# The first search's thresholds, the late parts of w2 and the fourth token plane of an attention and mixture-of-experts kernel

## The chip, the core and the metric

The kernel runs on one core of a Trainium2 chip. The core has five engines that work in parallel, each through its own list of instructions in order: TensorE (PE; its weight loads are PEld), VectorE (DVE), ScalarE (ACT), GpSimd (POOL) and SyncE (SP), which here only issues DMAs. The metric is the device time of one execution in microseconds (us), as the median of several.

## The reference

Attention over 8 batches, 12 heads, 448 tokens and 64 columns a head, then a mixture of 8 experts in which each (token, expert) pair is taken greedily by its logit until an expert has 448 tokens.

```python
scores = cap * np.tanh(scale * np.matmul(q, k.transpose(0, 1, 3, 2)) / cap)
attn = softmax(scores); x = matmul(attn, v)            # 3584 tokens, 768 columns
logits = x @ w_gate                                     # 8 experts
for idx in np.argsort(-logits.flatten()):               # greedy, best first
    tok, e = idx // E, idx % E
    if assigned[tok] >= 0 or counts[e] >= N // E: continue
    assigned[tok] = e; counts[e] += 1
for e in range(E):
    h = np.maximum(x[assigned == e] @ w1[e], 0.0)       # 768 -> 1024
    out[assigned == e] = h @ w2[e]                      # 1024 -> 768
```

## The kernel before, in words

**Two stages.** The first 338 us are attention, with the logits of each batch behind it. Then the experts are found one after another, each by a *search*, and each found expert gets a *pass* p of two matrix products. The first search (`s.cur==0`) runs before any pass; the later ones run beside the passes. The same expert order as in the reference comes out.

**A search** finds three thresholds, one after another: A, B and C, with 5, 6 and 5 steps in the first search. A step (`select`, L498 to L517) has three thresholds and counts how many of the 3584 x 8 candidates (128 x 224) lie below each: ACT takes one threshold (`cmpA`, L501, a Sign with a sum), DVE two (`cmpD`, L504, a compare with a sum). PE sums the counts over the partitions (L509), DVE adds up the terms of the row whose counts are within the limit (`fl`, L513), which gives the new base `th`, and then writes the next row of thresholds as base plus constants (`r_HA` from `r_CA`, L517). During the first search, ACT also evacuates the transposed rows of the last attention batches (`raw`, L50), POOL scales them (`xn`, L53) and SP stores them to `xs` in DRAM. The end of a search is a chain on DVE: `wt`, `wB`, `sx` (L573 to L578), then the expert's number `ei` (L612), and, at its end, `zz` (L658) behind which POOL gathers the expert's 448 rows (L789, four gathers of 128 rows, the last of 64). PE keeps itself busy meanwhile with small matmuls into a spare PSUM tile `psX` (`warm`, L714, columns 0 to 127).

**Proposals** (L449 to L468, DVE) make from the logits the next candidates `r_VA`, `r_VB`, `r_VC` and `r_K` for the search that follows; PE turns them (L478) and DVE moves the turned ones to SBUF (L483).

**A pass** is 320 ticks, one for each matmul: 144 for `ffn1` (8 blocks of 18, line L869), then 176 for `ffn2` (u=0 to 7: 24, 24, 24 and 16 matmuls, twice, line L900). Float32 values are cut into a high part (`w1h`, `w2h`, `xgh`: ACT, L760 or L821) and a low part (`w1l`, `w2l`: POOL, L764; `xgl`: POOL L828 or DVE L823); PE multiplies high by high, high by low and low by high. `cut` issues both parts. A pass needs eight parts of w2, n=0 to 7; the early ones are cut during `ffn1`, the rest (n=5, 6, 7, or only 7 for p=2) during `ffn2`, at the tick given by the table that the diff shows last. A `gap` memset (L762) stands between two splits of POOL.

**Tokens of the next expert** (for passes from FT=2 on) come in by planes: four ACT copies `pl` (L811) split the gathered rows in 16-bit planes, each is stored to DRAM `xz` (L812, on ACT's DMA queue), and two DMA transposes issued by SP (L815) bring the columns back: the first reads `xz0` (planes 1 and 2), the second `xz1` (planes 3 and 4). Then `cutt` makes `xgh` and `xgl` in four steps.

**The order** of each engine's instructions is the order in which the code is written, with the helpers `tick`, `xq` (a list of things to issue at a due tick) and `bg` (cuts that may be issued in idle time between two bounds) deciding where a piece stands. Nothing reorders it afterwards. A search's steps are issued between the matmuls of a pass by their own rule of ticks.

Of the kernel before, what the change touches and what calls it, by code (L numbers as in the profile page):

```python
# [7 lines left out]
AF=mybir.ActivationFunctionType; ALU=mybir.AluOpType; AX=mybir.AxisListType  # L8
# [324 lines left out]
class Routing:  # L333
# [155 lines left out]
    def select(s,wp,Vt,ab,mid=None,post=None):  # L489
        nc=s.nc; v=nc.vector  # L490
        NV=s.NV; wide=s.cur>1
        R=s.R8[ab] if wide else (4,)*s.steps[ab]
        T0,H,C=(s.T8,s.H8,s.C8) if wide else (s.T0,s.H,s.C)
        T0=T0[ab]; H=H[ab]; C=C[ab]; steps=len(R)
        th=[T0[:,k:k+1] for k in range(R[0]-1)]
        for i in range(steps):
            m=R[i]-1; alone=s.cur>FT and ab=="A" and i<3; na=m if alone else 5 if m==7 else s.na
            cd=(s.cd8 if m==7 else s.cds)[s.nd%3]; s.nd+=1  # L498
            o=wp.tile([128,s.NX],BF16,name="cmpA",bufs=1)
            with nc.allow_low_precision(reason="integers up to 256 are exact in bfloat16"):  # L500
                for k in range(na,m): nc.scalar.activation(o,Vt,AF.Sign,bias=th[k],scale=-1.0,accum_out=cd[:,k:k+1])  # L501
                for k in range(na):
                    o=wp.tile([128,NV],BF16,name="cmpD",bufs=2)
                    with s.tc.issue_after(s.hold) if s.hold else nullcontext(): v.tensor_scalar(o,Vt[:,:NV],th[k],None,op0=ALU.is_lt,op1=ALU.add,accum_out=cd[:,k:k+1])  # L504
            if mid and i<len(mid): mid[i]()
            s.bg()
            s.pos='A'; yield max(6,12-s.since()) if s.cur==1 and s.since()<20 else 16 if m==7 and s.place()>304 else max(13,18-s.since()) if m==7 and s.since()<20 else s.hA+1*(s.cur==1)+(3 if m==7 else 0)+(3 if alone and i else 0); s.pos=''
            ps=s.psum()
            nc.tensor.matmul(ps[:,:m+1],s.bo,cd,start=True,stop=True)  # L509
# [3 lines left out]
            v.scalar_tensor_tensor(fl[:,:m+1],ps[:,:m+1],s.lim,H[:,i,0:m+1],op0=ALU.is_le,op1=ALU.mult,accum_out=t0)  # L513
            if i+1<steps:
                nt=wp.tile([128,1],F32,name="nt",bufs=2)
                m=R[i+1]-1
                v.tensor_scalar(H[:,i+1,m:2*m],C[:,i+1,0:m],t0,None,op0=ALU.add,op1=ALU.add,accum_out=nt)  # L517
                th=[t0]+[H[:,i+1,m+k:m+k+1] for k in range(1,m)]
            if i==steps-1:
                s.tA=t0  # L520
                if ab=="C": s.row(s.tA)
            s.pos='B'; yield s.hB; s.pos=''
    def search(s,wp,turned=()):
        nc=s.nc; v=nc.vector
        post=None
        if turned:
            for h in range(s.NC//16):
                if ("VA",h) not in turned: s.turn("VA",h)
            late=[lambda: s.propose_b(s.NC-4,s.NC,PB(nc)),lambda: None,lambda: s.key(s.NC-4,s.NC)]
            post=lambda: s.flips(s.pm.tile([128,512],F32,name="psM"))  # L530
        else: late,post=s.turns()
# [25 lines left out]
        k2=s.vps[:112,448:448+s.NC]  # L557
# [7 lines left out]
        if s.cur>=EW:  # L565
            yield 4
            s.pw=s.psum()
            nc.tensor.matmul(s.pw[:112,0:16],s.onesf,R,start=True,stop=True)
            s.best(wp,0,s.pw[:112,0:8],k2); s.pw=s.pw[:112,8:16]
        else:  # L570
            s.pw=part[0]; s.warm(4)
        tt=wp.tile([112,8],F32,name="wt")
        v.tensor_tensor(tt,s.pw,s.wm,op=ALU.mult)  # L573
        s.wB=wp.tile([112,1],F32,name="wB")
        v.tensor_reduce(s.wB,tt,axis=AX.X,op=ALU.max)
# [111 lines left out]
def ffn_all(nc, tc, ctx, rt, xs, xz, w1, w2, out, ident, E, wp, deferred, xctx, gen):  # L687
# [20 lines left out]
    m=0  # L708
    wu=[None]; end=[-99]
    def warm(n,t=None):  # L710
# [4 lines left out]
    rt.warm=warm; rt.since=lambda: now[0]-end[0]; rt.place=lambda: now[0]%320  # L715
    warm(9)
    step()
    units(2)
# [31 lines left out]
    def load2(p,n,gate=None):  # L750
# [6 lines left out]
    def cut(key,r,shape,name,bufs,eng=None,view=lambda t:t,use=lambda t:t):  # L757
        h=ws.tile(shape,F32R,name=name+"h",bufs=bufs)
        l=ws.tile(shape,F32R,name=name+"l",bufs=bufs)
        nc.scalar.activation(view(h),r,AF.Copy)  # L760
        if not eng:
            if tt[0]: nc.gpsimd.memset(gap,0.0)  # L762
            lp[0]=False; tt[0]=True
        (eng or nc.gpsimd).tensor_tensor(view(l),r,view(h).bitcast(F32),op=ALU.subtract)  # L764
        spl[key]=(use(h),use(l))
    def split1(p,f,eng=None):
        if p>=E: return
        cut((p,1,f),raw[p,1,f],[128,DC,128],"w1",3,eng)
    def split2(p,n):
        hf,i=order(p)[n]  # L770
        view=use=lambda t:t.rearrange("p (o d) -> p o d",o=2)
        cut((p,2,hf,i),raw[p,2,hf,i],[128,2*HD],"w2",8,None,view,use)
# [35 lines left out]
    def planes(j):  # L808
        o,n=TS[j]; k,r=divmod(j,2)
        pl=fp.tile([128,2,DM],I16,name="pl",bufs=4)  # L810
        nc.scalar.activation(pl[:n],row(j,n).bitcast(I16).rearrange("p (d h) -> p h d",h=2),AF.Copy)  # L811
        nc.scalar.dma_start(xz[k][r*256:r*256+2*n].rearrange("(p h) d -> p h d",h=2),pl[:n])  # L812
        if r:
            n=o+n-2*128*k
            nc.sync.dma_start_transpose(xgp[k][:,:DC*n].bitcast(I16).rearrange("p (c t) -> p c t",c=DC),xz[k])  # L815
    def cutt(p,k,c0,c1):
        newx(p)
        o,n=((0,256),(256,192))[k]
# [20 lines left out]
    def tick(n=1):  # L839
        cnt[0]+=n; bc[0]+=n; now[0]+=n  # L840
        if bc[0]>=BG:
            if pend: bc[0]=0; scatter(*pend.pop(0))
        if len(res)>cur[0]+1 and cur[0]+1 not in xgs:
            bc[0]=0; n=cur[0]+1; gather(n)
            if n>=FT:
                xq.extend((now[0]+TD+TJ*j,lambda j=j: planes(j)) for j in range(4))
                xq.extend(((n-1)*320+248+8*f,lambda f=f: split1(n,f)) for f in range(2))
                o=(n-1)*320; g=now[0]-o; a=max(262,g+92); b=max(284,g+120)
                bg.extend((o+x,o+min(y,316),z) for x,y,z in ((a,a+18,lambda: cutt(n,0,0,3)),(a,a+34,lambda: cutt(n,0,3,6)),(b,b+(4 if n==FT else 26),lambda: cutt(n,1,0,3)),(b,b+22,lambda: cutt(n,1,3,6))))
        while xq and xq[0][0]<=now[0]: xq.pop(0)[1]()  # L850
# [78 lines left out]
    for p in range(E):  # L929
# [22 lines left out]
        for u in range(8):  # L952
# [72 lines left out]
```

## Time and profile before

| what | value |
|---|---|
| median of 3 runs | 896.42 us (895.92 to 897.0) |
| the profiled execution, time and span | 895.64 us, 893.8 us |
| TensorE, mean granted clock | 1.000 |
| PE, share of the span | 96% |
| first search, first to last `fl` | 339.9 to 362.7 us |
| gather of the first expert | 370.3 us |
| `w2l` on POOL | 64 x 1.85 us = 118.0 us |

A row of the profile's views gives start and duration in us, engine, line, operation, the tile written <- the tiles read, shape, and in brackets how long the engine was idle before it and what it waited for. The rows are quoted where the prediction uses them.

### The profile page before, as it was taken

The page shows a single profiled execution, that of the slowest core. Times are in us where ns is not written, and L with a number is a line of the kernel's source. Part 1 is how long each engine was busy: PE and PEld are TensorE (multiplying, and loading weights), DVE is VectorE, ACT ScalarE, POOL GpSimd, SP SyncE. Part 2 cuts the span into 40 slices and gives each one's busy share as a digit, 9 for nine tenths or more (in the row PEclk, how much of TensorE's full clock was granted, in tenths as well). Part 3 has the DMA queues.
Part 4 walks back from the last instruction along what each step waited for, and adds up shares of the span by engine and source line. Part 5 has one row for each costly group of instructions (what it writes and reads, how often), then busy time and mean ns, then how long its engine had stood idle before and what let it go on. Part 6 is the DMA issues. An engine that isn't in the chain of part 4 may idle for free.

```text
span 893.8 us, 17555 instructions
## 1 busy us (share of the span) xinstructions
PE 861.8 (96%) x6198; PEld 629.2 (70%) x6198; DVE 595.9 (67%) x2020; ACT 583.9 (65%) x822; POOL 371.8 (42%) x528
## 2 busy tenths in 40 slices
PE   7899999999999997899999999999999999999997
PEld 4334444444333335788989989989889989999997
DVE  3788988989887888767777677777767772130210
ACT  6988898889899957274383683664645735425521
POOL 8100000000000007574585593683864855856941
PEclk9999999999999999999999999999999999999999
DMA  8799999997995007770931874846926927828601
GB/s 121 114 131 144 129 170 171 142 166 105 213 179 85 1 4 250 237 227 1 314 94 51 247 234 128 253 150 195 285 86 186 283 63 211 284 75 250 205 10 54
DMA packets 336121, 139.61 MB, mean 156 GB/s; under 512 B 258304, under 2 KB 325632, under 8 KB 335520
## 3 DMA queue, kind: packets, MB, share of 16 engines
q1 hardware_dynamic: 326448, 107.96, 55.5%
q0 software_dynamic: 4656, 22.02, 7.2%
q10 hardware_dynamic: 4928, 8.49, 2.6%
q8 instruction: 49, 0.80, 0.4%
q14 instruction: 40, 0.33, 0.1%
HBM read 97.15 MB, written 33.03 MB: 146 GB/s over the span
## 4 chain that ended last, share of the span: by engine, by line
PE 70%; issue 12%; DVE 6%; POOL 4%; DMA 3%; SPq 2%; ACT 2%; POOLq 0%; DVEq 0%; ACTq 0%
PE psH L869 23%; PE psH L900 14%; PE psA L189 12%; PE psS L148 10%; PE psM L206 4%; POOL xg L789 2%; PE psS L153 2%; SPq L92 2%; PE psM L37 1%; DVE es L165 1%; POOL w2l L764 1%; POOL out_dram L882 1%; DVE cmpD L504 1%; DMA xg<-xz 1%; DMA k<-in_k_dram 1%
## 5 line engine op out<-in xcount | busy, mean ns | idle before, releaser
L900 PE MATMUL psH<-w2h,hh 128*128 128x384 f32 x896 | 235.2, 340 | 0.0
L900 PE MATMUL psH<-w2l,hh 128*128 128x384 f32 x512 | 167.5, 341 | 3.6 <-POOL gap L762 3.6
L154 ACT ACTIVATE e<-psS 128x896 f32<-128x896 f32 x168 | 147.5, 909 | 30.8 <-PE psS L148 18.0
L900 PEld LDWEIGHTS psH<-w2h,hh 128*128 128x128 f32 x896 | 161.8, 188 | 0.3
L159 ACT ACTIVATE e<-e,bias 128x1792 f32<-128x1792 f32 (+2 forms) x74 | 147.3, 1991 | 2.0
L869 PE MATMUL psH<-xgh,w1h 128*128 128x448 f32 x384 | 143.2, 373 | 1.0 <-ACT xgh L821 0.7
L869 PE MATMUL psH<-xgh,w1l 128*128 128x448 f32 x384 | 141.4, 368 | 0.0
L148 PE MATMUL psS<-tq,tk 64*64 64x448 f32 x1152 | 129.9, 544 | 7.4 <-ACT e L154 4.8
L869 PE MATMUL psH<-xgl,w1h 128*128 128x448 f32 x384 | 136.7, 369 | 0.0
L764 POOL TENSOR_TENSOR w2l<-w2r,w2h 128x768 fp32r<-128x768 f32 x64 | 118.0, 1846 | 42.7 <-ACT w2h L760 42.7
L460 POOL TENSOR_SCALAR r_Bt<-r_b 112x4 f16<-112x4 int32 x1 | 0.2, 201 | 304.1 <-DVE rin L243 304.1
L764 POOL TENSOR_TENSOR w1l<-w1r,w1h 128x768 fp32r<-128x768 f32 x62 | 114.3, 1845 | 19.0 <-ACT w1h L760 14.3
L189 PE MATMUL psA<-e,nv 64*64 64x448 f32 x1104 | 120.5, 540 | 1.2 <-DVE xT L199 1.2
L165 DVE TENSOR_TENSOR es<-es,e 64x896 f32<-64x896 f32 (+2 forms) x74 | 100.3, 1356 | 2.6 <-ACT e L159 1.3
L900 PEld LDWEIGHTS psH<-w2l,hh 128*128 128x128 f32 x512 | 95.5, 188 | 5.7 <-POOL gap L762 5.6
L148 PEld LDWEIGHTS psS<-tq,tk 64*64 64x64 f32 x1152 | 43.7, 132 | 73.2 <-issue 37.9
L875 ACT ACTIVATE hh<-psH 128x448 fp32r<-128x448 f32 x64 | 34.8, 543 | 86.0 <-PE psH L869 79.7
L877 DVE SCALAR_TENSOR_TENSOR hh<-psH,hh 128x64 fp32r<-128x64 f32 (+1 forms) x128 | 43.9, 385 | 67.0 <-ACT hh L875 66.0
L189 PEld LDWEIGHTS psA<-e,nv 64*64 64x64 f32 x1104 | 46.4, 133 | 59.1 <-issue 49.6
L906 ACT ACTIVATE on<-psH 128x384 f32<-128x384 f32 x48 | 23.4, 487 | 90.2 <-PE psH L900 85.9
L869 PEld LDWEIGHTS psH<-xgh,w1h 128*128 128x128 f32 x384 | 72.5, 189 | 6.6 <-ACT xgh L821 1.0
L869 PEld LDWEIGHTS psH<-xgh,w1l 128*128 128x128 f32 x384 | 72.3, 188 | 5.2
(340 smaller groups left out, 1321.5 us busy)
## 6 DMA issues: line engine op xcount, KB each, us to landing
w1r<-in_moe_w_dram SPq DMA_DIRECT2D x64, 384.0 KB, 4.7
w2r<-in_moe_w_dram SPq DMA_DIRECT2D x64, 384.0 KB, 6.8
k<-in_k_dram SPq DMA_DIRECT2D x92, 112.0 KB, 3.4
q<-in_q_dram SPq DMA_DIRECT2D x92, 112.0 KB, 3.9
nv<-in_v_dram SPq DMA_DIRECT2D x72, 128.0 KB, 3.9
xz<-pl ACTq DMA_DIRECT2D x18, 384.0 KB, 3.0
xs<-xn SPq DMA_DIRECT2D x4, 1344.0 KB, 7.0
xs<-xn SPq DMA_DIRECT2D x4, 896.0 KB, 5.2
```

The lines of the kernel that those rows point to most:

```text
L148: for c in range(2): nc.tensor.matmul(ps[c*64:c*64+64,h,:S],tks[g,0][hp,o,u*128+c*64:u*128+c*64+64],tks[g,1][hp,o,:],start=True,stop=True)
L154: nc.scalar.activation(ev(g,r),ps[:,:,:S],AF.Tanh,scale=sr[0])
L159: act=lambda: nc.scalar.activation(e,e,AF.Exp,scale=sr[1],bias=bias)
L165: t=es_t[g]; add=lambda o,a,b: nc.vector.tensor_tensor(o,a,b,op=ALU.add)
L189: nc.tensor.matmul(avp[g,o][h*64:h*64+64,:S],lhs,rhs[hp,h,:],start=(j==0 and x==0),stop=j==3)
L206: nc.tensor.matmul(ps[g*32:g*32+32,:S],lhs,rhs,start=first,stop=last)
L764: (eng or nc.gpsimd).tensor_tensor(view(l),r,view(h).bitcast(F32),op=ALU.subtract)
L869: nc.tensor.matmul(ps[:,:C],a[:,c,:],b[:,c,:],start=(m==0),stop=(m==DC*3-1)); m+=1
L875: nc.scalar.activation(h[:,:C],ps[:,:C],AF.Relu)
L877: nc.vector.scalar_tensor_tensor(h[:,d:d+b-a],ps[:,a:b],0.0,h[:,a:b].bitcast(F32),op0=ALU.max,op1=ALU.subtract)
L900: nc.tensor.matmul(ps[:,:HD],h[:,f,a:a+128],spl[p,2,hf,f//2][w][:,f%2,:],start=(m==0),stop=(m==nm-1))
L906: if t<3: nc.scalar.activation(ons[p][0][:,t*DM+hf*HD:t*DM+hf*HD+HD],ps[:,:HD],AF.Copy)
```

## The change

It has four parts. (1) The late w2 parts of a pass p>1 are issued earlier: their high parts at ticks 6, 12 and 18 of the first `ffn2` unit (for p=2 the one late part at tick 2 of the second), and their low parts through `xq`, at ticks 188, 198 and 208 of the pass. (2) In the first search, all steps but the first of each pass have DVE subtract the base from the proposals and compare with constants, which ACT copied to columns 128 on of `psX` before the search; the row of thresholds is written behind the compares, and ACT's threshold is now the base itself. (3) The fourth plane's store is issued by SP, and both transposes behind it; the due times of the cuts move by a few ticks. (4) In the later searches `wt` is written to eight spare columns of the PSUM tile that already holds `psR`.

```diff
@@ Routing.select: one pass of a threshold search
+                quick=s.cur==0 and i>0
-                for k in range(na,m): nc.scalar.activation(o,Vt,AF.Sign,bias=th[k],scale=-1.0,accum_out=cd[:,k:k+1])
-                for k in range(na):
+                for k in [0] if quick else range(na,m): nc.scalar.activation(o,Vt,AF.Sign,bias=th[k],scale=-1.0,accum_out=cd[:,k:k+1])
+                for k in range(1,m) if quick else range(na):
                     o=wp.tile([128,NV],BF16,name="cmpD",bufs=2)
+                    if quick:
+                        v.scalar_tensor_tensor(o,Vt[:,:NV],t0,s.cps[ab][:,i,k:k+1].broadcast_to([128,NV]),op0=ALU.subtract,op1=ALU.is_lt,accum_out=cd[:,k:k+1])
+                        continue
...
+            if quick: v.tensor_scalar(H[:,i,m:2*m],C[:,i,0:m],t0,None,op0=ALU.add,op1=ALU.add,accum_out=wp.tile([128,1],F32,name="nt",bufs=2))
...
-                nt=wp.tile([128,1],F32,name="nt",bufs=2)
+                if s.cur: nt=wp.tile([128,1],F32,name="nt",bufs=2)
                 m=R[i+1]-1
-                v.tensor_scalar(H[:,i+1,m:2*m],C[:,i+1,0:m],t0,None,op0=ALU.add,op1=ALU.add,accum_out=nt)
+                if s.cur: v.tensor_scalar(H[:,i+1,m:2*m],C[:,i+1,0:m],t0,None,op0=ALU.add,op1=ALU.add,accum_out=nt)
@@ Routing.search
+        if s.cur==0:
+            ps=s.spare(); s.cps={}; o=128
+            for n in "ABC":
+                S=s.steps[n]; s.cps[n]=ps[:,o:o+3*S].rearrange("p (s k) -> p s k",k=3); o+=3*S
+                nc.scalar.activation(s.cps[n][:,1:],s.C[n][:,1:],AF.Copy)
...
-            s.best(wp,0,s.pw[:112,0:8],k2); s.pw=s.pw[:112,8:16]
+            s.best(wp,0,s.pw[:112,0:8],k2); tt=s.pw[:112,16:24]; s.pw=s.pw[:112,8:16]
         else:
-            s.pw=part[0]; s.warm(4)
-        tt=wp.tile([112,8],F32,name="wt")
+            s.pw=part[0]; s.warm(4); tt=wp.tile([112,8],F32,name="wt")
@@ ffn_all, cut and split2
-        if not eng:
-            if tt[0]: nc.gpsimd.memset(gap,0.0)
-            lp[0]=False; tt[0]=True
-        (eng or nc.gpsimd).tensor_tensor(view(l),r,view(h).bitcast(F32),op=ALU.subtract)
+        def low():
+            if not eng:
+                if tt[0]: nc.gpsimd.memset(gap,0.0)
+                lp[0]=False; tt[0]=True
+            (eng or nc.gpsimd).tensor_tensor(view(l),r,view(h).bitcast(F32),op=ALU.subtract)
+        if at is None: low()
+        else: xq.append((at,low)); xq.sort(key=lambda x: x[0])
@@ ffn_all, planes
-        nc.scalar.dma_start(xz[k][r*256:r*256+2*n].rearrange("(p h) d -> p h d",h=2),pl[:n])
-        if r:
-            n=o+n-2*128*k
-            nc.sync.dma_start_transpose(xgp[k][:,:DC*n].bitcast(I16).rearrange("p (c t) -> p c t",c=DC),xz[k])
+        (nc.sync if j==3 else nc.scalar).dma_start(xz[k][r*256:r*256+2*n].rearrange("(p h) d -> p h d",h=2),pl[:n])
+        if j==3:
+            for k,n in ((0,256),(1,192)): nc.sync.dma_start_transpose(xgp[k][:,:DC*n].bitcast(I16).rearrange("p (c t) -> p c t",c=DC),xz[k])
@@ ffn_all, tick: due times of the cuts of the token columns
-                o=(n-1)*320; g=now[0]-o; a=max(262,g+92); b=max(284,g+120)
-                bg.extend((o+x,o+min(y,316),z) for x,y,z in ((a,a+18,lambda: cutt(n,0,0,3)),(a,a+34,lambda: cutt(n,0,3,6)),(b,b+(4 if n==FT else 26),lambda: cutt(n,1,0,3)),(b,b+22,lambda: cutt(n,1,3,6))))
+                o=(n-1)*320; g=now[0]-o; a=max(262,g+92); b=max(284,g+118)
+                bg.extend((o+x,o+min(y,316),z) for x,y,z in ((a,a+18,lambda: cutt(n,0,0,3)),(a,a+34,lambda: cutt(n,0,3,6)),(b,b+(0 if n==FT else 26),lambda: cutt(n,1,0,3)),(b,b+(7 if n==FT else 22),lambda: cutt(n,1,3,6))))
@@ ffn_all: the late w2 parts of a pass p>1
-                for m,n in ({3:[(2,7)]} if p==2 else {2:[(14,5),(20,6)],3:[(2,7)]}).get(u,()): wk[m]=wk.get(m,[])+[lambda n=n: split2(p,n)]
+                for m,n in ({1:[(2,7)]} if p==2 else {0:[(6,5),(12,6),(18,7)]}).get(u,()): wk[m]=wk.get(m,[])+[lambda n=n: split2(p,n,320*p+138+10*n)]
```

On VectorE, the list around the fourth and fifth step of pass C of the first search: before, and of the change (`psR` is the count from PE, `th` the base, `r_CC` the constants in SBUF, `r_HC` the row, `psX` the PSUM tile).

```order
L513 SCALAR_TENSOR_TENSOR fl,th<-psR,r_HC 128x4
L517 TENSOR_SCALAR r_HC,nt<-r_CC,th 128x3
L504 TENSOR_SCALAR cmpD,r_cd_316<-r_qt,th 128x224
L504 TENSOR_SCALAR cmpD,r_cd_316<-r_qt,r_HC 128x224
L513 SCALAR_TENSOR_TENSOR fl,th<-psR,r_HC 128x4
```

```order
L518 SCALAR_TENSOR_TENSOR fl,th<-psR,r_HC 128x4
L506 SCALAR_TENSOR_TENSOR cmpD,r_cd_316<-r_qt,th,psX 128x224 x2
L509 TENSOR_SCALAR r_HC,nt<-r_CC,th 128x3
L518 SCALAR_TENSOR_TENSOR fl,th<-psR,r_HC 128x4
L506 SCALAR_TENSOR_TENSOR cmpD,r_cd_317<-r_qt,th,psX 128x224 x2
L509 TENSOR_SCALAR r_HC,nt<-r_CC,th 128x3
L518 SCALAR_TENSOR_TENSOR fl,th<-psR,r_HC 128x4
```

The row of thresholds, which stood between `fl` and the compares, stands behind both compares, which no longer read it.

On ScalarE, pass p=3 from the last `hh` of `ffn1` to the first results of the second half: before, and of the change. `pl` are the plane copies, `xz` the planes in DRAM, `on` a result.

```order
L875 ACTIVATE hh<-psH 128x448 x3
L906 ACTIVATE on<-psH 128x384
L811 ACTIVATE pl<-xg_4110 128x1536
L812 DMA xz_62<-pl 128x1536
...
L906 ACTIVATE on<-psH 128x384
L811 ACTIVATE pl<-xg_4111 64x1536
L812 DMA xz_63<-pl 64x1536
L760 ACTIVATE w2h<-w2r 128x768 x2
L906 ACTIVATE on<-psH 128x384
L760 ACTIVATE w2h<-w2r 128x768
```

```order
L886 ACTIVATE hh<-psH 128x448 x3
L769 ACTIVATE w2h<-w2r 128x768 x3
L917 ACTIVATE on<-psH 128x384
L823 ACTIVATE pl<-xg_4113 128x1536
L824 DMA xz_62<-pl 128x1536
...
L824 DMA xz_63<-pl 128x1536
L917 ACTIVATE on<-psH 128x384
L823 ACTIVATE pl<-xg_4114 64x1536
```

Three high parts `w2h` (n=5, 6, 7), which stood behind the fourth copy and its store, stand ahead of the first `on`. POOL's list doesn't change in order: gathers, then the low parts.

On SyncE, the third pass around the transposes: before, and of the change.

```order
L747 DMA w1r<-in_moe_w_dram 128x6x128
L747 ISA
L747 DMA w1r<-in_moe_w_dram 128x6x128
L815 DMA_TRANSPOSE xg_4110<-xz_62 128x6x512
L815 DMA_TRANSPOSE xg_4111<-xz_63 128x6x384
L747 ISA
L747 DMA w1r<-in_moe_w_dram 128x6x128
L755 ISA
```

```order
L756 DMA w1r<-in_moe_w_dram 128x6x128
L756 ISA
L756 DMA w1r<-in_moe_w_dram 128x6x128
L824 DMA xz_63<-pl 64x1536
L826 DMA_TRANSPOSE xg_4113<-xz_62 128x6x512
L826 DMA_TRANSPOSE xg_4114<-xz_63 128x6x384
L756 ISA
```

The fourth plane's store came to SP's list ahead of both transposes, and is gone from ScalarE's. PE's list is the same instructions in the same order.

More of the change, by code (lines that the diff above doesn't have):

```diff
@@ L714, in warm @@
         for _ in range(n): nc.tensor.matmul(t[:,:128],ident,ident,start=True,stop=True)
-    rt.warm=warm; rt.since=lambda: now[0]-end[0]; rt.place=lambda: now[0]%320
+    rt.warm=warm; rt.spare=lambda: wu[0]; rt.since=lambda: now[0]-end[0]; rt.place=lambda: now[0]%320
     warm(9)
@@ L756, in load2, with cut @@
         raw[p,2,hf,i]=t
-    def cut(key,r,shape,name,bufs,eng=None,view=lambda t:t,use=lambda t:t):
+    def cut(key,r,shape,name,bufs,eng=None,view=lambda t:t,use=lambda t:t,at=None):
         h=ws.tile(shape,F32R,name=name+"h",bufs=bufs)
@@ L768, in split1, with split2 @@
         cut((p,1,f),raw[p,1,f],[128,DC,128],"w1",3,eng)
-    def split2(p,n):
+    def split2(p,n,at=None):
         hf,i=order(p)[n]
         view=use=lambda t:t.rearrange("p (o d) -> p o d",o=2)
-        cut((p,2,hf,i),raw[p,2,hf,i],[128,2*HD],"w2",8,None,view,use)
+        cut((p,2,hf,i),raw[p,2,hf,i],[128,2*HD],"w2",8,None,view,use,at)
     def early(p,ei):
```

## The prediction

> **What bounds the kernel now.** I read the engine table first, then the table of what each engine waited for, then the timeline at those places.
>
> ```profile
> span 893.8 us, 17555 instructions
> PE 861.8 (96%) x6198; PEld 629.2 (70%) x6198; DVE 595.9 (67%) x2020; ACT 583.9 (65%) x822; POOL 371.8 (42%) x528
> ```
>
> PE works 96% of the span, and the diff neither adds nor removes work on it. So there are only two things to win: the stretch in which PE waits for the first search (338 to 376 us), and PE's short waits in the expert passes (from 380 us on). All of the latter, from 470 us to the end, are three rows:
>
> ```profile
> PE psH L900 <- POOL gap L762: 3.6, 5, 1.2
> PE psH L869 <- ACT xgh L821: 0.7, 1, 0.7
> PE psR L618 <- DVE ei L612: 0.3, 2, 0.2
> ```
>
> (Time waited in all, times, longest.) The change aims at all three and at the first search. The profiled execution took 895.64 us (span 893.8), 0.78 below the median of 896.42; the sum below is made on 895.64 and then moved by 0.78. A measurement of this kernel tells about 0.2% (1.8 us) from no change.
>
> **The change, part 1: late w2 parts.** The five waits of L900 are for the last low parts (POOL, L764), and those wait for the high parts on ACT (L760). The fourth pass (p=3) shows the chain. ACT, then POOL, then PE (the second PE row is one of p=5):
>
> ```profile
> 607.57 0.55 ACT L875 ACTIVATE hh<-psH 128x448 fp32r<-128x448 f32 x1 [3.53 <-PE psH L869]
> 611.87 0.49 ACT L906 ACTIVATE on<-psH 128x384 f32<-128x384 f32 x1 [3.75 <-PE psH L900]
> 613.43 1.49 ACT L811 ACTIVATE pl<-xg 128x1536 int16<-128x1536 int16 x1 [1.07 <-DMA xg<-xs,idx]
> ...
> 621.59 1.58 ACT L760 ACTIVATE w2h<-w2r 128x768 fp32r<-128x768 f32 x2 [0.57 <-ACT pl L811]
> ```
>
> ```profile
> 614.70 0.09 POOL L762 MEMSET gap<- 1x1 f32 x1
> ...
> 622.51 1.86 POOL L764 TENSOR_TENSOR w2l<-w2r,w2h 128x768 fp32r<-128x768 f32 x1 [7.72 <-ACT w2h L760]
> ...
> 626.20 1.84 POOL L764 TENSOR_TENSOR w2l<-w2r,w2h 128x768 fp32r<-128x768 f32 x1
> ```
>
> ```profile
> 628.10 0.62 PE L900 MATMUL psH<-w2l,hh 128*128 128x384 f32 x2 [0.54 <-POOL gap L762]
> ...
> 755.78 0.61 PE L900 MATMUL psH<-w2l,hh 128*128 128x384 f32 x2 [1.18 <-POOL gap L762]
> ```
>
> ACT is idle for 3.75 us ahead of `on`, while the three high parts (0.8 us each: 1.58 for two) stand behind four plane copies. After the change they run there, from 608.1 to about 610.6, which ends before `on` needs ACT at 611.87, so that cover holds by 1.3 us. POOL's order stays as it is (gathers, then the three low parts), so the low parts start at the end of the gathers, 614.8, rather than at 622.5. Three of them at 1.85 us with gaps end at about 620.3 instead of 628.0. PE first missed one at 627.6 (628.10 − 0.54), so 7.7 us of lead cover it in every such pass. Two matmuls in a row show 0.62 us, so a matmul that starts behind another takes about 0.3 on its own and 0.17 more in a full stream; an interrupted stream therefore loses some 0.16 beyond the idle time shown. Five waits: 3.6 + 5 × 0.16 = **−4.4 us**. The plane copies don't start sooner (they wait for the gather: 1.07), and nothing else stands behind the moved parts. Bound: −4.4 to 0, and past 0 by what follows.
>
> **The price of part 1.** Low parts that start at 614.8 run beside the last steps of the proposals on DVE, where POOL was idle before:
>
> ```profile
> 614.61 0.42 DVE L463 TENSOR_TENSOR r_VC<-r_P,r_Ct 112x256 f16<-112x256 f16 x1
> 614.94 0.18 DVE L464 TENSOR_TENSOR r_K<-r_At,r_Bt 112x32 f32<-112x32 f16 x1
> 615.04 0.18 DVE L468 SCALAR_TENSOR_TENSOR r_K<-r_kk,r_Ct 112x32 f32<-112x32 f16 x1
> ...
> 615.98 0.39 DVE L483 CAST r_VAt<-psR 128x224 f16<-128x224 f32 x1 [0.75 <-PE psR L478]
> ...
> 618.70 0.16 DVE L513 SCALAR_TENSOR_TENSOR fl<-psR,r_H8A 128x4 f32<-128x4 f32 x1 [1.10 <-PE psR L509]
> ...
> 679.21 0.39 DVE L483 CAST r_VAt<-psR 128x224 f16<-128x224 f32 x1 [0.41 <-PE psR L478]
> ...
> ```
>
> ```profile
> 342.41 0.54 DVE L468 SCALAR_TENSOR_TENSOR r_K<-r_kk,r_Ct 112x4 f32<-112x4 f16 x1
> ...
> L578 DVE SCALAR_TENSOR_TENSOR sx<-wt,wB,r_e8c x7: 227/228/5410, 363.7 to 722.2; 112x8 f32<-112x8 f32 x7
> ...
> L504 DVE TENSOR_SCALAR_CACHE_REDUCE cmpD<-r_VAt,th x4: 442/443/448, 340.2 to 344.6; 128x224 bf16<-128x224 f16 x4
> ```
>
> A DVE operation with two SBUF operands is held up when POOL runs an elementwise operation: L468 takes 0.54 us rather than 0.18 at 342.41, under POOL's chain `xn`, and one `sx` of 0.23 took 5.41 us at 722.2, under a run of POOL splits. The compares (L504, one SBUF operand) stay at 0.44 throughout. So L464 and L468 can now be held for one low part, to the gap at about 616.7, that is 1.6 us late. The next DVE step has 0.75 us of slack behind PE's turn, and the first `fl` another 1.1. In p=3 a single hold costs PE 0 to 0.25 us; in p=4, where the turn is waited for 0.41 only, about 0.5. In p=2 just one low part stands there, and p=5 has no search behind it. A hold isn't certain, since L463, which reads two SBUF operands itself, is running when POOL asks at 614.8; I take +0.35, bounds 0 and the rival below.
>
> The Trainium skill, "SBUF — State Buffer", section "Who interferes with whom", says that a DVE instruction with two SBUF inputs contends with a GpSimd instruction that reads SBUF, and that whoever issues first holds the port for the whole instruction. The trace agrees (0.54, 5.41); the rule speaks against this move and not for a particular winner.
>
> **Part 2: first search.** One of its sixteen steps (the last) and the STT that the change will use in place of the compare:
>
> ```profile
> 361.24 0.16 DVE L513 SCALAR_TENSOR_TENSOR fl<-psR,r_HC 128x4 f32<-128x4 f32 x1 [0.27 <-PE psR L509]
> ...
> 361.44 0.22 DVE L517 TENSOR_SCALAR_CACHE_REDUCE r_HC<-r_CC,th 128x3 f32<-128x3 f32 x1
> ...
> 361.58 0.44 DVE L504 TENSOR_SCALAR_CACHE_REDUCE cmpD<-r_qt,th 128x224 bf16<-128x224 f16 x1
> ...
> 362.68 0.16 DVE L513 SCALAR_TENSOR_TENSOR fl<-psR,r_HC 128x4 f32<-128x4 f32 x1 [0.27 <-PE psR L509]
> ...
> L537 DVE SCALAR_TENSOR_TENSOR r_qt<-r_VAt,th,psM x1: 448/448/448, 345.9 to 345.9; 128x224 f16<-128x224 f16 x1
> ```
>
> Behind each `fl`, which gives the new base `th`, the row of thresholds (L517) delays the first compare by 0.14 us (361.58 − 361.44). In the changed order the compares come right behind `fl`, add the base themselves and read the constants from PSUM; the row goes behind them, into the 0.27 us in which DVE waits for PE. An STT with a PSUM operand on as many elements takes 0.448 against 0.44, so the compares cost the same. Thirteen steps get it (not the first of each pass): 13 × 0.14 = 1.8. ACT takes some of it back, since it counts one threshold in each step and copies one or two `raw` of the deferred attention batches:
>
> ```profile
> 338.70 0.51 ACT L501 ACTIVATE cmpA<-r_VAt,r_T0A 128x252 bf16<-128x252 f16 x1 [2.29 <-POOL r_Bt L460]
> ...
> 352.37 0.50 ACT L501 ACTIVATE cmpA<-r_qt,r_HB 128x252 bf16<-128x252 f16 x1 [0.32 <-DVE r_HB L517]
> ...
> 352.88 1.06 ACT L50 ACTIVATE raw<-psL 112x512 f32<-112x512 f32 x2
> ...
> 353.83 0.50 ACT L501 ACTIVATE cmpA<-r_qt,r_HB 128x252 bf16<-128x252 f16 x1
> ```
>
> A step with two copies keeps ACT busy for 1.46 us (353.83 − 352.37), more than the 1.44 of a step now (362.68 − 361.24) and than the 1.30 it is to become. ACT's compare is shorter than DVE's two by about 0.1, and a step with one copy gives ACT back what it lost (0.32 idle), so each of some five such steps loses perhaps 0.08: 1.8 − 0.4 = **−1.4 us**. Then what is late next: the gather.
>
> ```profile
> 349.21 3.07 POOL L53 TENSOR_TENSOR xn<-raw,rin 112x512 f32<-112x512 f32 x3 [1.10 <-DVE fl L513]
> ...
> 368.97 0.73 POOL L783 MEMSET xg<- 64x768 f32 x1 [4.57 <-DMA xs<-xn]
> ...
> 370.30 1.23 POOL L789 DMA_INDIRECT xg<-xs,idx  x1 [0.60 <-DVE zz L658]
> ```
>
> It waits for the search (`zz`) only 0.60 us longer than for the stored rows `xs` and the memset behind them. The store hangs on POOL's `xn` chain, which once waits 1.10 us for a step of the search; by then five or six shortened steps have passed (0.8), and the chain runs on without idle time. So `xs` comes 0.8 sooner too, and the end of the search can gain 0.60 + 0.8 = 1.4 before it is hidden: the cap just lets the gain through. Bounds: −0.6 (the store does not move) and −1.4; below that only if ACT or PE's transposes set the pace, then near 0. The three copies of the constants to PSUM fall to ACT before the first compare, where it waits 2.3 us anyway (338.70).
>
> **Part 3: fourth plane.** In the third pass (p=2) PE waits 0.7 for the last token columns:
>
> ```profile
> 500.40 0.54 ACTq L812 DMA_DIRECT2D xz<-pl  x1
> ...
> 506.26 0.83 ACT L821 ACTIVATE xgh<-xg 128x768 fp32r<-128x768 f32 x1
> ...
> 512.43 1.26 ACT L821 ACTIVATE xgh<-xg 128x576 fp32r<-128x576 f32 x2 [1.65 <-DMA xg<-xz]
> ```
>
> ```profile
> L815 SPq DMA_TRANSPOSE xg<-xz x2: 2652/3038/3424, 499.1 to 505.3; - x2
> DMA to landing us min/median/max: 7.1/7.1/7.1
> ```
>
> The store of the fourth plane was issued at 500.40 while the first transpose (from 499.1) was on its way, and the second transpose, which waits for it, started at 505.3 and landed 7.1 later. Now SP issues the store, then both transposes: the first starts some 1.9 us later (501.0), ends its issue at about 504.4 (3.4), and the second can follow there, 0.9 sooner, if the store is faster with the transposes behind it. I take **−0.7** of the 0.7 + 0.16 that can go; bounds −0.9 and +0.6 (the second transpose behind a first one that lands later). ACT's first cut of the token columns, formerly at 506.26, right after the first transpose (499.1 + 7.1), will wait 1 to 2 us for it; the columns of the second are cut 6 us later (512.43), so PE does not wait for that. In later passes PE doesn't wait here. The Trainium skill, "DMA: Bandwidth & Descriptors", section "Issuing engines are not separate DMA queues", says that DMAs of all issuers share the same 16 engines, so that another issuer saves only the time to initiate. By that rule the move is worth ACT's 0.54 us of issue, which no engine waits for, and this term would be 0. The rows above speak of an order of transfers rather than of a queue; which of the two it is, no run so far shows.
>
> **Part 4: `wt` in PSUM.** The `sx` of 5.41 us reads `wt` and a constant, both in SBUF; with `wt` in PSUM only one operand is left there, as in the compares, and the hold goes. PE waited for its result in L618: −(0.2 + 0.16), about **−0.3**; bounds 0 and −0.3.
>
> **Sum.** −4.4 + 0.35 − 1.4 − 0.7 − 0.3 = −6.45, or 889.2 us for the profiled execution and 890.0 by the median.
>
> **Rivals.**
> - *Part given back on DVE* (0.12). If L464 gets in at the first gap of POOL and L468 only at the second, DVE is 3.5 us late, less 0.75 (0.41) and about 0.9 of slack: 1.8 in p=3 and 2.2 in p=4, 3.65 more than taken: 893.6. For it: the `sx` of 5.41 missed two gaps. Against: other holds ended at one operation (0.54).
> - *Slower* (0.06). The same two operations miss all gaps and wait for all three low parts, to 620.3: 5.2 late, less the slack 3.5 and 3.9, thus 7.4 for the 0.35 taken, and the time is 897.1. It decides from the point at which L468 ends after about 619.9 in both passes; with part 3 or the search failing as well it goes past 898.2. For it: the 5.41, again. Against: it needs both passes, and L463 runs right ahead.
> - *The search or the transposes do not reach the end* (0.2): the store of `xs` doesn't move (−0.6 instead of −1.4), or the second transpose gains nothing (0 for −0.7): 890.7 to 891.5, with both.
> - *The forecast* (0.62): 889.2 to 890.7.
>
> The range takes in both ends of the search and the transposes and the first rival's price, and stops short of the slower one; below, it reaches to all best bounds (−7.0: 889.4) and the scatter of runs: 888.5 to 894.2. Faster by over 0.2% (under 894.6) 0.87; within 0.2% 0.09; slower 0.04.
>
> **What will show it.** Waits of PE: L900 behind POOL's gap gone (now 3.6); `w2h` ahead of `on` at 608 to 611, low parts from 614.8; if PE waits for `cmpD` or L483 right behind the proposals, the first rival. First search: `fl` to `fl` 1.30, DVE's idle time before `fl` near zero; if ACT's `cmpA` is what PE waits for, the 1.4 is too high. The gather at 368.9 rather than 370.3. Second transpose issued at 504.4, landing 511.5; if later than 512.4, the term has the wrong sign. `sx` never above 0.3. The forecast is wrong if PE shows new waits in its expert passes that sum to more than 2 us.

## The result and the profile after

The changed kernel takes **906.26 us** (905.19 to 906.74, 4 runs), the kernel before 896.17 us (895.36 to 897.0): a ratio of 1.0111 with an interval of 1.0093 to 1.0128. It is slower by 10 us; 890.0 was forecast. The profiled execution of it took 906.74 us.

The page of the changed kernel, its span and the row of the granted TensorE clock (40 slices of the span, in tenths):

```profile
span 905.0 us, 17573 instructions
...
PEclk9999999999999999999999899999999999999999
```

Where the row of before had only nines, one slice has an 8. What PE waited for from 470 us on (total, times, longest):

```profile
PE psR L514 <- DVE cmpD L508: 8.5, 2, 4.4
PE psH L880 <- ACT xgh L832: 3.2, 1, 3.2
PE psR L627 <- DVE ei L621: 0.2, 1, 0.2
```

(The changed file's L514, L880, L911 and L627 are L509, L869, L900 and L618 of before.) The waits of the FFN for POOL's low parts, 3.6 us before, are gone, as forecast. Two waits for VectorE of over 4 us have come, and the wait for `xgh` rose from 0.7 to 3.2. Since PE runs the same instructions in the same order in both kernels, the start of the same matmul in both traces gives a ledger. The column on the right is the best version of the experiments (e6), for later:

| place on PE, by the time of before | changed minus before, us | e6 minus before, us |
|---|---|---|
| transposes of gathered rows (376.0) | −0.2 | −0.3 |
| first matmul of the third pass (513.2) | +2.3 | −1.0 |
| 27 us into the third pass (540) | +5.0 | −1.0 |
| p=3, just ahead of the search's first count (618.3) | +4.85 | −1.3 |
| p=3, first count of the search (618.5) | +9.1 | −1.3 |
| p=3, 2 us on (620.3) | +10.6 | −1.3 |
| p=3, behind the late low parts (630) | +9.8 | −2.1 |
| p=4, first count (681.7) | +14.4 | −2.1 |
| p=4, 2 us on (683.9) | +15.8 | −2.1 |
| p=4, behind the late low parts (700) | +15.1 | −2.8 |
| p=5, behind them (780) | +12.8 | −5.1 |
| end | +11.2 | −6.7 |

**VectorE, p=3.** VectorE's and POOL's timelines of the changed kernel:

```profile
618.90 0.18 DVE L460 TENSOR_SCALAR r_Bt<-r_b 112x32 f16<-112x32 int32 x1
619.00 6.15 DVE L461 TENSOR_SCALAR r_Ct<-r_c 112x32 f16<-112x32 int32 x1
625.04 0.41 DVE L462 TENSOR_TENSOR r_VB<-r_P,r_Bt 112x256 f16<-112x256 f16 x1
```

```profile
618.42 1.13 POOL L801 DMA_INDIRECT xg<-xs,idx  x1 [0.30 <-issue]
619.55 0.09 POOL L773 MEMSET gap<- 1x1 f32 x1
619.60 1.85 POOL L775 TENSOR_TENSOR w2l<-w2r,w2h 128x768 fp32r<-128x768 f32 x1
621.38 0.09 POOL L773 MEMSET gap<- 1x1 f32 x1
621.43 1.86 POOL L775 TENSOR_TENSOR w2l<-w2r,w2h 128x768 fp32r<-128x768 f32 x1
623.22 0.09 POOL L773 MEMSET gap<- 1x1 f32 x1
623.27 1.80 POOL L775 TENSOR_TENSOR w2l<-w2r,w2h 128x768 fp32r<-128x768 f32 x1
```

An operation of 0.18 us stands for 6.15, and ends with the third low part (625.07). Neither gap let VectorE in. The same row shows 2.51 in p=2, where one low part follows the gathers, and 6.14 and 6.17 in p=4 and p=5.

**The clock.** PE's granted clock behind that wait, in windows of 2 us (busy time and count of each engine, then PEclk, DMA share, GB/s):

```profile
624.00:626.00 2.00, 0.00 (x0) 0.00 (x0) 2.00 (x6) 1.86 (x2) 1.10 (x2) 1.00 0.50 197
626.00:628.00 2.00, 0.42 (x6) 0.42 (x5) 1.67 (x10) 0.00 (x0) 0.00 (x0) 0.89 0.43 91
628.00:630.00 2.00, 2.00 (x9) 2.00 (x8) 2.00 (x13) 0.00 (x0) 0.00 (x0) 0.50 1.02 223
630.00:632.00 2.00, 2.00 (x10) 2.00 (x9) 0.78 (x6) 0.49 (x1) 0.00 (x0) 0.76 1.09 224
632.00:634.00 2.00, 2.00 (x13) 1.84 (x13) 1.03 (x7) 0.00 (x0) 0.00 (x0) 1.00 1.06 213
```

After a wait of 4.1 us PE runs for some 3 us at half its clock. That is the further 1.5 us (9.1 to 10.6) in the ledger. In p=4 the wait is 4.4 us and the further loss 1.4 (14.4 to 15.8).

**Third pass.** SyncE's two transposes, POOL's first scatter of results (with the same row of before under it), ScalarE's first cut of the second transpose's columns, and PE:

```profile
500.95 6.98 SPq L826 DMA_TRANSPOSE xg<-xz  x2
```

```profile
504.80 1.02 POOL L893 DMA_INDIRECT out_dram<-on,idx  x1
```

```profile
505.81 1.03 POOL L882 DMA_INDIRECT out_dram<-on,idx  x1 [0.15 <-ACT on L906]
```

```profile
514.68 0.68 ACT L832 ACTIVATE xgh<-xg 128x576 fp32r<-128x576 f32 x1 [4.33 <-DMA xg<-xz]
```

```profile
515.42 0.74 PE L880 MATMUL psH<-xgh,w1h 128*128 128x448 f32 x1 [3.16 <-ACT xgh L832]
...
517.32 0.57 PE L880 MATMUL psH<-xgh,w1h 128*128 128x448 f32 x1
```

The second transpose was issued earlier, as forecast (504.7 for 505.3; 504.4 was forecast), and landed 2.3 us later: 9.9 us from issue to landing, not 7.1. PE waited 3.16 us, and its matmuls then take 0.57 us for 0.36: half clock again, 2.7 us more.

### The profile page after: what moved, and what is told of

It is laid out like the page before. It is cut to its first block, busy times and chain, and to the rows that moved or that the text cites. A ratio compares the mean times of both kernels' runs of the same rounds, so it can differ in the third digit from the quotient of the medians.

```text
span 905.0 us, 17573 instructions
## 1 busy us (share of the span) xinstructions
PE 865.7 (96%) x6198; PEld 634.3 (70%) x6198; DVE 611.4 (68%) x2020; ACT 584.0 (65%) x825; POOL 371.8 (41%) x528
## 4 chain that ended last, share of the span: by engine, by line
PE 81%; DVE 8%; issue 3%; DMA 3%; SPq 2%; ACT 2%; POOL 0%; POOLq 0%; DVEq 0%; ACTq 0%
PE psH L880 26%; PE psH L911 21%; PE psA L189 12%; PE psS L148 10%; PE psM L206 4%; PE psS L153 2%; SPq L92 2%; PE psM L37 1%; DVE r_Ct L461 1%; DMA xg<-xz 1%; DVE es L165 1%; DVE cmpD L508 1%; DMA k<-in_k_dram 1%; PE psL L37 1%; ACT e L154 1%
## 5 line engine op out<-in xcount | busy, mean ns | idle before, releaser
L911 PE MATMUL psH<-w2h,hh 128*128 128x384 f32 x896 | 236.9, 342 | 0.0
L911 PE MATMUL psH<-w2l,hh 128*128 128x384 f32 x512 | 166.9, 341 | 0.0
L911 PEld LDWEIGHTS psH<-w2h,hh 128*128 128x128 f32 x896 | 163.6, 190 | 0.1
L880 PE MATMUL psH<-xgh,w1h 128*128 128x448 f32 x384 | 144.5, 376 | 3.5 <-ACT xgh L832 3.2
L880 PE MATMUL psH<-xgh,w1l 128*128 128x448 f32 x384 | 142.7, 372 | 0.0
L880 PE MATMUL psH<-xgl,w1h 128*128 128x448 f32 x384 | 137.4, 371 | 0.0
L911 PEld LDWEIGHTS psH<-w2l,hh 128*128 128x128 f32 x512 | 96.8, 190 | 0.1
L880 PEld LDWEIGHTS psH<-xgh,w1h 128*128 128x128 f32 x384 | 73.3, 191 | 9.1 <-ACT xgh L832 3.5
L880 PEld LDWEIGHTS psH<-xgh,w1l 128*128 128x128 f32 x384 | 73.2, 191 | 5.3
```

The source lines that it names most:

```text
L880: nc.tensor.matmul(ps[:,:C],a[:,c,:],b[:,c,:],start=(m==0),stop=(m==DC*3-1)); m+=1
L911: nc.tensor.matmul(ps[:,:HD],h[:,f,a:a+128],spl[p,2,hf,f//2][w][:,f%2,:],start=(m==0),stop=(m==nm-1))
```

## The experiments

Twelve kernels. Those marked "one run" have one time. The kernel before gave 897.6 us beside e1 to e4, 896.6 beside e5 to e8 and 900.0 beside e9 to e12 (medians), with single runs from 894.7 to 903.1 (and one of 2190.3, left out): it varies more than the best versions do.

### e1: the late w2 parts as before

```diff
-                for m,n in ({1:[(2,7)]} if p==2 else {0:[(6,5),(12,6),(18,7)]}).get(u,()): wk[m]=wk.get(m,[])+[lambda n=n: split2(p,n,320*p+138+10*n)]
+                for m,n in ({3:[(2,7)]} if p==2 else {2:[(14,5),(20,6)],3:[(2,7)]}).get(u,()): wk[m]=wk.get(m,[])+[lambda n=n: split2(p,n)]
```

> The changed kernel with only part 1 taken back: the late w2 parts are cut at the ticks of before. Theory (hold): PE's waits of 4.3 and 4.6 us in the passes p=3 and p=4 come from VectorE held at L461 by the low parts that follow the gathers. Then L461 is never above 0.3 us, both waits are gone, the five waits of L900 for POOL are back (3.6 us), and the time is 896.2 + 4.85 (third pass, as in the changed kernel) - 0.3 (wt) = about 900.8 us. Rival (the holds are not POOL's: the search's new code or wt in PSUM makes VectorE late): L461 stays at 6 us and the time at 905 or more.

Measured: 895.61 us (894.03 to 898.18); ratio to before 0.997 (0.9951 to 0.9989). L461 takes 0.2 us again; PE's waits:

```profile
PE psH L880 <- ACT xgh L832: 1.9, 1, 1.9
PE psH L911 <- POOL gap L773: 1.7, 2, 0.9
PE psR L514 <- DVE cmpD L508: 0.2, 1, 0.2
```

The two waits for VectorE (4.1 and 4.4 us by PE's rows, 4.3 and 4.6 by the ledger) are gone, so they came with the moved parts. The time is 5.2 us under the expectation. Some 3.4 of it are the third pass, on which this edit does nothing: it cost only 1.5 us in this profile, since the transpose took 8.5 us, PE waited 1.9 and kept its clock. That loss, then, is not a fixed amount. The rest is part of the expectation that fell: of the five waits of L900 for POOL (3.6 us) only two came back (1.7).

### e2: the fourth plane's store as before

```diff
-        (nc.sync if j==3 else nc.scalar).dma_start(xz[k][r*256:r*256+2*n].rearrange("(p h) d -> p h d",h=2),pl[:n])
-        if j==3:
-            for k,n in ((0,256),(1,192)): nc.sync.dma_start_transpose(
+        nc.scalar.dma_start(xz[k][r*256:r*256+2*n].rearrange("(p h) d -> p h d",h=2),pl[:n])
+        if r:
+            n=o+n-2*128*k
+            nc.sync.dma_start_transpose(
...
```

The due times of the cuts are those of before again.

> The changed kernel with only part 3 taken back: the fourth plane is stored by ScalarE, each transpose is issued behind its second store, due times of the cuts as before. Theory (order on one queue): the second transpose lands some 6.6 us after the first has landed, and the first was late because it stood behind the fourth plane's store. Then the first lands near 505.8, the second near 512.4, PE waits 0.7 us there at full clock, and the time is 906.3 - 5.05 = 901.2 us. Rival (the loads and scatters beside the transposes made them slow): landing stays near 514 and the time above 904 us.

Measured: 904.63 us (901.76 to 908.38; the profile is of the slowest run). The expectation fell: the second transpose was issued at 506.0, landed 9.8 us later, and PE waited 4.1 us. Its store had landed late enough (505.9) for a scatter of POOL to go out at 505.89, 0.1 ahead. In the profile of before the scatter followed the transpose by 0.55 us. So neither the store's queue nor its place explained the third pass; the scatter became the suspect.

### e3: low parts behind the proposals

`K2` is `r_K`, which L468 writes last among the proposals.

```diff
-                if tt[0]: nc.gpsimd.memset(gap,0.0)
+                if at: nc.gpsimd.tensor_copy(gap,rt.T["K2"][0:1,0:1])
+                elif tt[0]: nc.gpsimd.memset(gap,0.0)
```

> The changed kernel with one thing added: ahead of each late low part POOL copies one element of r_K, so that it waits until VectorE has finished the proposals (L468). Theory (hold): low parts start about 0.2 us behind L468, VectorE is never held, L900 never waits for them, PE has no wait above 0.5 us in p=3 and p=4 and no loss of clock there; 896.2 + 4.85 (third pass) - 4.4 (L900) - 0.3 (wt) = about 896.4 us. Rival (VectorE is late for another reason): L461 near 6 us again and 904 us or more.

Measured: 893.14 us (890.58 to 894.92), ratio 0.9941 (0.9919 to 0.9962). POOL's row shows the wait that was put in:

```profile
618.73 0.18 POOL L773 COPY gap<-r_K 1x1 f32<-1x1 f32 x1 [0.65 <-DVE r_K L468]
618.88 1.85 POOL L776 TENSOR_TENSOR w2l<-w2r,w2h 128x768 fp32r<-128x768 f32 x1
```

A wait of 0.65 us on POOL takes 13 us off the changed kernel; some 2.5 of them are the third pass, which lost less in this run's profile (2.8 us for 5.2). All that PE still waited for was the third pass (2.0 us) and `ei` (0.2); L900's waits are gone too. Part 1 is worth its gain once its low parts start behind L468.

### e4: the search's constants in a PSUM tile of their own

```diff
-            ps=s.spare(); s.cps={}; o=128
+            ps=s.pm.tile([128,512],F32,name="psM"); s.cps={}; o=0
```

> The changed kernel with the constants of the first search in a PSUM tile of their own (the free second psM) and not beside the columns that the warming matmuls write. Theory (shared tile): the compares' waits for psX matmuls (0.38 us in the last step) go, the last fl of the first search comes at 361.4 instead of 361.8 (before: 362.7), and PE starts its first transposes of gathered rows 0.3 us sooner; time 905.9 us. Rival (ScalarE sets the pace of steps with two raw copies): the last fl stays at 361.8 and the time at 906.3 us.

Measured: 906.29 us (905.37 to 907.39). The rival holds: the compares' waits for `psX` matmuls go, and the time does not move.

### e5: as e3, and no scatter beside the transposes

```diff
-            if pend: bc[0]=0; scatter(*pend.pop(0))
+            if pend and not (cur[0]==1 and 560<now[0]<640): bc[0]=0; scatter(*pend.pop(0))
```

> The kernel of the run with low parts behind the proposals, and in addition no result is scattered in the last 80 ticks of pass p=1, in which the transposes for the third pass run (the scatters come at the start of p=2). Theory (collision): the second transpose is slow (8.5 to 9.9 us to landing in the runs so far, 7.1 in the profile of before) when a scatter of POOL is issued at the same moment; without one it lands 7 us or less after its issue, at about 512, PE waits under 0.8 us there, the clock stays at 1.00, and the time falls from 893.1 to about 890.0 us. Rival (the transpose is slowed by the weight loads, or varies by itself): landing at 8.5 us or more after issue, PE waits 2 us or more, time near 893 us.

Measured: **889.46 us** (888.78 to 889.82), ratio 0.9905 (0.9874 to 0.9936). The first scatter goes at 513.08, behind the second transpose's landing; the second transpose lands 6.6 us after its issue, ScalarE takes it at 512.10:

```profile
512.10 0.69 ACT L833 ACTIVATE xgh<-xg 128x576 fp32r<-128x576 f32 x1 [1.10 <-DMA xg<-xz]
```

```profile
513.08 1.39 POOL L894 DMA_INDIRECT out_dram<-on,idx  x1 [0.15 <-issue]
```

### e6: as e5, with the fourth plane's store as before

The diffs of e2, e3 and e5 together.

> As the run with low parts behind the proposals and no scatter beside the transposes, but with part 3 taken back (store by ScalarE, each transpose behind its second store). Theory (collision): with no scatter beside it the second transpose takes 7 us here too, from 505.3 or 506.0, PE waits 0.7 to 1.2 us, 890.5 us: the store on SP is worth under 0.7 us by itself. Rival (the order store, first, second transpose matters by itself): 2 us or more between this run and the one with the store on SP.

Measured: **889.49 us** (888.85 to 889.84), ratio 0.9908 (0.9878 to 0.9939): the same as e5. The second transpose took 6.0 us.

All fourteen profiles together, for the second transpose of the third pass:

| scatter of POOL | profiles | issue to landing, us |
|---|---|---|
| within 0.25 us of its issue | changed, e1, e2, e3, e4, e7, e8, e9 | 8.4 to 9.9 |
| 0.55 us behind its issue | before | 7.1 |
| none before it has landed | e5, e6, e10, e11, e12 | 6.0 to 6.6 |

### e7: `r_VB` ahead of `r_Ct`

```diff
-        v.tensor_scalar(w("Ct"),...)
         v.tensor_tensor(w("VB"),...)
+        v.tensor_scalar(w("Ct"),...)
```

> The changed kernel with one pair of VectorE's proposal operations exchanged: r_VB (L462, two SBUF operands) now stands ahead of r_Ct (L461, one SBUF operand, int32 to f16). Theory (the moment decides): whatever stands there when POOL takes the port is held: r_VB shows 6 us in p=3 and p=4, r_Ct 0.2. Rival (the form decides): r_VB takes 0.4 as before and r_Ct behind it 5.6 us. Time 906 us either way.

Measured (one run): 907.81 us.

```profile
618.53 0.18 DVE L460 TENSOR_SCALAR r_Bt<-r_b 112x32 f16<-112x32 int32 x1
618.75 6.26 DVE L461 TENSOR_TENSOR r_VB<-r_P,r_Bt 112x256 f16<-112x256 f16 x1
624.93 0.17 DVE L462 TENSOR_SCALAR r_Ct<-r_c 112x32 f16<-112x32 int32 x1
```

Now `r_VB` is held, from 0.69 us after the start of the fourth gather (618.06); in the changed kernel it was `r_Ct`, from 0.58 us. So `r_VB` is held where it stands first, and the rival falls. POOL's first low part shows its start only at 619.24, so the hold begins some 0.5 us ahead of the start on the record, while the gather still stands there. Whether `r_Ct`, with one SBUF operand, was held itself, or its row is long because `r_VB` was held right behind it, the two runs don't settle. The trace of e4 says something on it: `gt` (L615, one SBUF tensor and one column of scalars) stands there for 1.09 us at 363.28 under `xn`, instead of 0.23, with another operation of its kind behind it. So a hold does not seem to need two SBUF tensors.

### e8: longer gaps ahead of every late low part

```diff
-                if tt[0]: nc.gpsimd.memset(gap,0.0)
+                if tt[0]:
+                    for _ in range(6 if at else 1): nc.gpsimd.memset(gap,0.0)
```

> The changed kernel with six gap memsets in place of one ahead of each late low part (0.3 to 0.5 us of them). Theory (the gap is too short): VectorE gets in at the first longer gap, no operation is held longer than 2.5 us, PE's waits in p=3 and p=4 fall from 4.3 and 4.6 to about 1 us or less and the clock is kept: 896 us. Rival (POOL keeps the port over everything that it has ready): L461 stays at 6 to 7 us and the time at 906 us or more.

Measured (one run): 891.99 us; no operation held. But not for the reason expected:

```profile
616.51 0.82 POOL L774 MEMSET gap<- 1x1 f32 x6
617.34 1.85 POOL L776 TENSOR_TENSOR w2l<-w2r,w2h 128x768 fp32r<-128x768 f32 x1
```

The gap ahead of the first low part moved its start behind L468 (616.87 to 617.05), as e3 does with a wait. VectorE never stood before a gap, so this says nothing of one between two low parts.

### e9: longer gaps between the low parts only

The loop of e8, for the second and third low part only (and for the single one of p=2).

> The changed kernel with six gap memsets (0.8 us, as the run with longer gaps showed) ahead of the second and third late low part only; the first follows the gathers as in the changed kernel. Theory (the port is POOL's from the moment a low part is next, and a longer gap gives it back): VectorE is held at L461 or L462 for the first low part only, 2.5 us as in p=2 of the changed kernel, and PE waits under 1 us in p=3 and p=4, no loss of clock there. Rival (once held, until all that POOL has ready is done): L461 8 us (6.2 and two gaps of 0.8), PE waits of 6 us.

Measured (one run): 893.87 us.

```profile
616.28 2.52 DVE L461 TENSOR_SCALAR r_Ct<-r_c 112x32 f16<-112x32 int32 x1
618.70 0.41 DVE L462 TENSOR_TENSOR r_VB<-r_P,r_Bt 112x256 f16<-112x256 f16 x1
```

```profile
616.88 1.85 POOL L776 TENSOR_TENSOR w2l<-w2r,w2h 128x768 fp32r<-128x768 f32 x1
618.67 0.82 POOL L774 MEMSET gap<- 1x1 f32 x6
```

The theory holds: VectorE gets in as soon as a gap of 0.82 us begins, and is held 2.52 us instead of 6.15. PE's two waits for VectorE sum to 1.3 us. In the changed kernel a gap of one memset, 0.09 us, did not do that.

### e10: as e6, without the quick steps

```diff
-                quick=s.cur==0 and i>0
+                quick=False
```

The row of thresholds stands behind `fl` again, and the copies of the constants are left out.

> The kernel of the run with low parts behind the proposals, no scatter beside the transposes and the store as before (889.5 us), with part 2 taken back as well: the first search as before. Theory (the gather path swallows it): the last fl comes 1.0 us later, PE's first transposes of gathered rows only 0.2 to 0.4 us later, time 889.8 us. Rival (the steps count in full): 890.5 to 890.9 us.

Measured: 889.86 us (889.41 to 890.52), beside 889.47 (888.93 to 890.21) for its control e12. Part 2 is worth some 0.4 us at most: the difference is smaller than the scatter of either kernel's runs.

### e11: as e6, with one load ahead of the first gather

```diff
-    WG=3; NW=23; WJ=4
+    WG=1; NW=23; WJ=4
```

> The kernel of the run with the store as before (889.5 us), with only one load of w1 instead of three ahead of the first gather; the two others wait for the gather's token, as the fourth does. Theory (the gather shares the DMA engines with the loads): the first gather, 5.5 to 5.8 us from issue to landing so far, lands in 4.5 us, PE's transposes start 0.8 us sooner, time 888.7 us unless ffn1 then waits for the later loads. Rival (the gather's own time, not the loads): landing 5.5 us after issue, time 889.5 us or more.

Measured: 893.35 us (892.63 to 893.75). PE's first transposes of gathered rows began 5.3 us after the gather's issue. In e6 and e12, the same kernel with the loads ahead, it was 5.9 and 5.8, and 5.5 to 6.4 in the others. So the theory is half right: with fewer loads the rows came some 0.5 us sooner, in this one profile. PE then waited 3.2 us for the postponed weights, which cost more than that.

### e12: e6 again

> The kernel of the run with low parts behind the proposals, no scatter beside the transposes and the store as before, once more, as the control for the two runs beside it: 889.5 us.

Measured: 889.47 us (888.93 to 890.21), ratio 0.9885 (0.986 to 0.991).

## Why the prediction was wrong

The failed step is **the price of part 1**. Its mechanism was named (VectorE held where POOL's low parts run beside the proposals), but it was priced at +0.35 us, by letting VectorE in at the first gap. The row that said otherwise was quoted: the `sx` of 5.41 us had missed two gaps. Measured was a hold over all three low parts (6.15 us, changed kernel), and over one where a gap of 0.82 us followed it (2.52 us, e9). It also began sooner than taken: at `r_Ct` (L461, 0.6 us ahead of the first low part's start on the record) or at `r_VB` behind it, where the prediction had VectorE already in `r_VC` (L463). The Trainium skill, "SBUF — State Buffer", section "Who interferes with whom", says that the engine that issues first has the shared ports for the whole instruction and the other one is blocked. These runs show VectorE blocked for three such instructions in a row.

The prediction's other side had rows too. VectorE does get in at times: the `r_K` at 342.41 (0.54 us) was let in behind one of eight `xn` that ran without a gap, and another `sx` of before took 0.34 us, let in at a single memset with the next split right behind it. POOL's rows for both, and that `sx`:

```profile
339.86 8.24 POOL L53 TENSOR_TENSOR xn<-raw,rin 112x512 f32<-112x512 f32 x8 [0.43 <-ACT raw L50]
...
657.68 1.82 POOL L764 TENSOR_TENSOR w1l<-w1r,w1h 128x768 fp32r<-128x768 f32 x1
659.45 0.09 POOL L762 MEMSET gap<- 1x1 f32 x1
659.50 1.84 POOL L764 TENSOR_TENSOR w2l<-w2r,w2h 128x768 fp32r<-128x768 f32 x1
```

```profile
659.19 0.34 DVE L578 SCALAR_TENSOR_TENSOR sx<-wt,wB,r_e8c 112x8 f32<-112x8 f32 x1
```

So the runs show that the late low parts held VectorE (e1, e3) and that a longer gap ends the hold (e9). What decides whether it gets in at a short gap or at none stays open.

The rival on the slower side had this case: both passes held to the end, with waits of 3.5 and 3.9 us, at 897.1. Measured were 4.1 and 4.4 (in the ledger 4.85 to 9.1 and 9.8 to 14.4). What it lacked is **the clock**, which no term of the prediction had: behind each of them PE ran at half clock, 1.5 and 1.4 us more.

The second failed step is **part 3**. The second transpose was issued sooner, as said, but its landing was taken to follow the issue by 7.1 us. That figure was one run with a scatter 0.55 us behind. The change also frees ScalarE of the store, so its `w1h` cut starts at 500.06, 1 us sooner (501.04 before), POOL's two splits with it, and the scatter behind them went out at 504.80 instead of 505.81, on top of the transpose. Instead of −0.7 the pass lost 5.2 us in the profile, half of it to the clock. With the scatters out of the way the store on SP is worth nothing (e5 and e6: 889.46 and 889.49). The Trainium skill, "DMA: Bandwidth & Descriptors", section "Issuing engines are not separate DMA queues", says that another issuing engine saves only the time to initiate a DMA. These two runs agree.

Point by point, the rest:

- **Part 1's gain** was right. L900 waits for nothing; in e6's ledger its five waits give about 5 us for the 4.4 forecast.
- **Part 2** was mis-sized: −1.4 forecast, −0.4 at most measured (e10). The last `fl` came 0.85 us sooner (361.83 for 362.68). Behind it the gain shrank: `sx` was held for 1.07 instead of 0.73 us by `xn`, so the gather was issued only 0.5 us sooner, and PE's transposes of its rows started only 0.2 sooner. The cap had been worked out to the gather's issue and not to its landing. Why the rows come later behind the issue stays open; e11 suggests that the loads beside the gather are a part of it.
- **Part 4** was right: `sx` is at 0.23 us in all later searches, and PE's place in the ledger moves by −0.3 where PE had waited for `ei` (729.7 of before; 0.3 forecast).
- **The sum**: the versions without the two collisions (e5, and e6, which has no part 3) give 889.5 where 890.0 was forecast for the change, so the two collisions cost 17 us. That 889.5 is so near is partly luck: part 1 gave more than forecast, part 2 less, and what the third pass gained (0.7 us in e6's ledger) came from the moved scatters, which are not in the change.

```profile
L587 DVE SCALAR_TENSOR_TENSOR sx<-psR,wB,r_e8c x6: 226/226/227, 421.4 to 737.3; 112x8 f32<-112x8 f32 x6
...
L587 DVE SCALAR_TENSOR_TENSOR sx<-wt,wB,r_e8c x1: 1065/1065/1065, 362.9 to 362.9; 112x8 f32<-112x8 f32 x1
```

Those are the six later searches with `wt` in PSUM, and the first with it in SBUF.

## What to carry to other kernels

When work is moved into idle time of one engine, price what it does to an engine that it can hold up by the whole run of instructions that will be ready, and start it by a wait behind any short chain that the bound engine waits for: 0.65 us of waiting on POOL were worth some 10 here. A step that leaves an engine free sooner pulls forward everything behind it, here a scatter onto a transpose, so the DMAs that it releases count as part of the change. Here every wait of PE of 1.95 us or more in the passes also cost clock, so the price of such a wait is more than its length.

## What the runs showed of the hardware

- Several short POOL instructions that are ready one behind the other can hold VectorE as one: 6.15 us for three of 1.85 with memsets of 0.09 between, 2.52 where the second gap was 0.82. They do not always: the `sx` at 659.19 of before took 0.34.
- A wait of PE of 1.9 us left the clock at 1.00 (1.91 in e1, 1.87 in e8). Waits of 1.95 (e9) and 2.04 us (e3) took it to 0.50 for about 3.4 us. The wait's length does not set how long that lasts: in the changed kernel one of 3.2 us cost 6.8 us of half clock, those of 4.1 and 4.4 cost 3.4 each. In e3:

```profile
516.00:518.00 2.00, 2.00 (x10) 1.74 (x9) 1.71 (x8) 1.48 (x4) 1.20 (x3) 0.69 1.12 340
518.00:520.00 2.00, 2.00 (x7) 1.78 (x6) 1.74 (x10) 1.93 (x5) 2.00 (x3) 0.50 1.07 363
520.00:522.00 2.00, 2.00 (x12) 1.66 (x11) 0.43 (x2) 1.01 (x2) 2.00 (x3) 0.96 1.11 364
```

The Trainium skill, "TensorE: Matmul & The Clock Gate", section "Why this matters for your kernels", advises against idle gaps of over about 3 us. Here 2.0 us were enough, so that figure is no safe bound for this kernel; 1.91 and 1.95 lie too close together to be a bound either.

- A DMA transpose that is issued within 0.25 us of an indirect scatter takes 8.4 to 9.9 us to land (eight profiles), 7.1 with one 0.55 us behind it, and 6.0 to 6.6 without one (five profiles).
